# Attention followed by an MLP on one core: W1's first load and the first matmuls by contraction tile, and half of the first M built on ScalarE

## The chip, the cores and the metric

The kernel runs on one core of a Trainium2 chip. The metric is device microseconds of one execution. A kernel is profiled once per run and timed several times; the profile's span is some 1.8 us shorter than the time of the same execution (299.0 us against 300.83 for the kernel before), since it begins with the first recorded instruction. Times inside a profile count from the span's start.

## The reference

```python
def _attn_ref(q, k, v):                      # q, k, v: (8, 8, 576, 64), batch, head, position, feature
    q_s = softmax of q over features         # exp, then divided by its sum
    k_s = softmax of k over positions
    kv  = einsum('bhsd,bhse->bhde', k_s, v)  # 64 x 64 per head
    return einsum('bhsd,bhde->bhse', q_s, kv)

def _moe_ref(x, w_in, w_out):                # x: (4608, 512), w_in: (512, 2048), w_out: (2048, 512)
    h = x @ w_in
    g = where(h > 0, h, exp(min(h, 0)) - 1)  # ELU
    return g @ w_out
```

(The two softmaxes are shortened here.) Nearly all the work is in the two products of the MLP.

## The kernel before

The program lists operations with what they read and write, and a small scheduler gives each engine its order. Here the order is fixed by a table, `ORDER`, of operation numbers per engine. The work comes in *units* of four heads of one batch; units 0 and 1 fill the first block of 512 columns of x. For one unit:

- ScalarE takes exp of q and k; VectorE sums exp of q (`ZQ`) and scales it (`QS`); V is cast (`VB`).
- TensorE transposes QS; the result is copied out of PSUM as `qsT`.
- TensorE multiplies K by V, with a column of ones for K's sums. *M* (`MBLK`) is that product divided by the sums, laid out with each pair of heads on a block diagonal. *A* is M times `qsT`, copied out of PSUM as x, transposed (`XT`, called X below).
- The MLP then multiplies `W1` by X in groups g = 0 to 7 of two 128-row tiles each, over four *contraction tiles*, kc = 0 to 3. Unit 0 makes kc 0 and 1, unit 1 makes kc 2 and 3.

```python
    def m(self, n, ps, key, at=KV):                  # M of unit n, on VectorE
        S.add("dve", 82, lambda e: e.reciprocal(rz..., PV[:, :, D:D + 1]), ...)
        for h in range(2):
            hs = slice(h * 64, h * 64 + 64)
            S.add("dve", 208, lambda e, h=h, hs=hs: e.tensor_tensor(
                self.MBLK[i][hs, :, h:128:2], PV[hs, :, 0:D],
                rz[hs, :].unsqueeze(2).broadcast_to([64, 2, D]), ALU.mult), ...)
    # ... cut ...
    def program(self):
        # ... loads of q, k, v of units 0 and 1 ...
        for g0, g1, half in ((0, 3, 0), (0, 3, 1), (3, 5, None), (5, 8, None)):
            self.load_w1(g0, g1, half, ...)          # two transfers each
        # ... cut: attention of units 0 and 1, W2's loads ...
        for half in range(2):                        # the first matmuls of the MLP
            for g in range(3):
                self.hg_mm(0, g, turns[g], key, half)   # 2 tiles x 2 contraction tiles
        for g in range(8):
            self.hg(0, g, turns[g], key, "da"[g % 2], g > 2)   # groups 3 to 7, and all ELUs
```

Where TensorE would sit idle early on, a routine puts *filler* matmuls: they write to a bank that nothing reads yet, and are there to keep TensorE's clock up. It begins with them at a fixed time.

```python
    SPIN_FROM = 7900.0      # ns
    # ... in fill(), for each idle stretch of TensorE before the MLP:
    count = int((o.start - free - 150) / (430 if free == self.SPIN_FROM else 260))
```

The softmax here doesn't subtract the row's maximum and nothing guards it: scores larger than these inputs give would overflow.

Of the kernel before, what the change touches and what calls it, by code (L numbers as in the profile page):

```python
# [11 lines left out]
B, H, S, D = 8, 8, 576, 64  # L12
# [11 lines left out]
    "pe": (  # L24
        "30 28 32 43 45 47 50 67 54 68 70 71 69 72 82 86 93 115 103 90 129 128 137 136 131 139 107 "
        "130 138 109 151 152 150 126 134 149 132 156 157 158 140 173 146 153 159 172 174 175 233 238 "
        "237 239 192 243 249 245 244 251 250 201 255 257 256 203 263 262 212 268 261 267 269 313 309 "
        "321 317 350 220 325 333 329 280 391 334 282 338 342 291 412 346 351 299 399 404 395 417 362 "
        "400 364 408 425 430 373 413 421 438 426 381 479 434 439 487 450 500 492 483 505 488 452 513 "
        "518 461 496 469 501 526 509 564 514 572 522 538 585 527 540 568 577 573 598 581 586 590 594 "  # L30
        "603 611 549 607 636 599 556 657 640 612 662 644 649 653 645 670 622 666 624 683 688 658 679 "
        "632 675 671 634 696 709 684 692 701 714 697 705 722 727 735 718 710 740 731 748 723 744 761 "
        "736 766 757 753 749 770 787 762 774 779 775 783 788 792 793 805 797 801 809 "),
    "act": (
        "3 22 33 23 24 31 29 34 35 48 44 55 73 76 77 79 83 84 87 94 95 97 104 91 92 116 117 119 98 "
        "108 120 127 135 133 163 160 179 147 166 154 169 205 176 230 231 188 234 180 240 241 191 246 "
        "215 252 253 202 258 204 211 264 213 265 273 270 214 218 310 322 314 217 284 318 221 279 326 "
        "294 355 281 330 296 335 283 290 392 343 297 292 339 293 347 366 352 376 300 405 361 396 378 "
        "363 401 409 365 372 418 375 443 414 454 379 422 374 431 427 382 464 435 449 480 440 451 466 "
        "493 467 484 531 489 453 460 463 506 519 462 497 470 502 542 510 515 565 537 523 539 554 551 "  # L40
        "528 569 578 574 541 552 616 582 591 587 595 548 555 550 608 637 600 626 557 604 641 613 650 "
        "654 621 646 623 663 667 689 631 625 659 680 633 676 672 685 693 715 702 698 635 706 719 728 "
        "711 732 741 724 745 737 767 758 750 771 754 763 776 780 784 789 794 798 806 802 810 812 "),
    "dve": (
        "2 4 5 0 6 7 25 26 37 27 38 39 40 41 42 36 46 49 51 52 53 56 74 75 78 80 81 85 88 89 96 100 "
        "105 106 101 102 122 118 110 111 112 123 124 141 142 143 148 155 182 183 184 177 178 232 206 "
        "235 236 193 194 207 195 196 197 242 208 247 198 248 254 259 260 266 274 275 271 272 276 311 "
        "312 285 319 222 223 286 320 224 225 226 227 287 327 328 356 331 332 357 336 337 358 344 345 "
        "348 349 367 353 368 354 301 369 302 303 304 305 306 397 398 402 403 410 411 444 415 416 445 "
        "446 423 424 428 429 383 384 455 385 386 387 388 436 456 457 437 441 442 485 490 486 532 491 "  # L50
        "498 499 533 471 503 472 534 473 474 504 511 543 544 512 475 476 516 517 524 525 545 529 530 "
        "570 571 575 576 583 584 596 597 617 588 618 589 609 610 601 558 602 619 642 643 559 627 560 "
        "561 562 614 615 628 629 563 655 656 647 648 668 669 660 661 673 674 681 682 686 687 694 695 "
        "707 699 708 700 720 721 712 713 733 734 725 726 746 747 738 739 759 760 751 752 772 764 765 "
        "773 777 778 785 786 "),
    "gp": (
        "1 14 15 16 17 18 19 20 21 57 59 58 63 60 61 62 64 66 99 65 113 125 144 121 114 145 181 186 "
        "189 "),
    "sp": (
        "8 9 10 11 12 13 170 187 161 164 171 185 165 190 200 168 162 199 209 210 216 167 219 277 278 "  # L60
        "229 228 323 315 288 295 316 289 324 298 341 359 308 360 377 307 340 393 370 371 406 394 420 "
        "380 407 419 447 433 390 465 482 432 458 448 389 494 481 495 459 468 478 507 520 535 477 567 "
        "508 521 536 553 566 546 580 547 579 620 605 638 606 593 592 630 651 652 639 677 665 690 664 "
        "678 703 716 717 691 730 704 729 756 768 769 742 755 743 782 781 790 791 795 796 799 800 807 "
        "808 803 804 811 "),
}
# [173 lines left out]
def t_f32r(n):  # L240
    return (n + 32) / 2.4


class Gen:
# [49 lines left out]
    def init(self):  # L294
        S = self.S
        S.add("dve", 100, lambda e: e.memset(self.ID[:, :], 0.0), -95, W=["ID"])
        S.add("gp", 300, lambda e: e.affine_select(
            self.ID[:, :], self.ID[:, :], compare_op=ALU.not_equal, fill=1.0, base=0,
            pattern=[[-1, 128]], channel_multiplier=1), -38, X=["ID"])
        self.ident = S.ops[-1]  # L300
        S.add("dve", 60, lambda e: e.memset(self.RZK[0][:, :], 0.0), -90, W=["RZK0"])
        S.add("act", 1400, lambda e: e.activation(self.RZK[0][:, :], self.RZK[0][:, :], AF.Exp), -80,
              X=["RZK0"])
        self.table = S.ops[-1]
        for i in range(2):
            S.add("dve", 80, lambda e, i=i: e.memset(self.VB[i][:, :, :, D:D + 1], 1.0), -88,
                  W=[f"VBone{i}"], follow=S.ops[-1] if i else None)
            S.add("dve", 280, lambda e, i=i: e.memset(self.MBLK[i][:, :, :].bitcast(F32), 0.0), -88,
                  W=[f"MBLK{i}", f"MBLK{i}0", f"MBLK{i}1"], follow=S.ops[-1])
        self.cleared = S.ops[-1]  # L310
# [18 lines left out]

    def load_w1(self, g0, g1, half, key, after=()):  # L330
        w = self.w_in.rearrange("(h kc d) f -> h d kc f", h=2, d=D)
        sl = slice(g0 * 256, g1 * 256)
        ks = slice(0, 4) if half is None else slice(2 * half, 2 * half + 2)
        xs = (0, 1) if half is None else (half,)
        for h in range(2):
            self.S.add("gp", ISSUE["gp"], lambda e, h=h: e.dma_start(
                self.W1[h:128:2, ks, sl], w[h, :, ks, sl]), key,
                W=[f"W1_{g}{x}{h}" for x in xs for g in range(g0, g1)],
                dma=f"w1{g0}{xs[0]}{h}", nbytes=(len(xs) * (g1 - g0) << 17) * (1.25 if g0 == 3 else 1), after=after,
                follow=self.gpq)  # L340
            self.gpq = self.S.ops[-1]

    def load_w2(self, s, key, after=()):
# [106 lines left out]
    def kv_mm(self, n, ps, at=KV):  # L450
# [3 lines left out]
        def mm(e):  # L454
# [7 lines left out]
            return last  # L462
        return 615 if at == self.KV else 290, [f"kR{i}", f"VB{i}", f"VB{i}x", f"VBone{i}"], mm

    def m(self, n, ps, key, at=KV):
# [5 lines left out]
        for h in range(2):  # L471
            hs = slice(h * 64, h * 64 + 64)
            S.add("dve", 208, lambda e, h=h, hs=hs: e.tensor_tensor(  # L473
                self.MBLK[i][hs, :, h:128:2], PV[hs, :, 0:D],
                rz[hs, :].unsqueeze(2).broadcast_to([64, 2, D]), ALU.mult),
                key, R=[f"RZK{i}"], W=[f"MBLK{i}{h}"], X=banks)

# [4 lines left out]
    def ao_mm(self, n, x, ps, at=0):  # L482
# [5 lines left out]
        def mm(e):  # L488
            for f in range(2):
# [4 lines left out]
        return (2 * t_f32r(n_), [f"qsT{self.alt(n)}{y}" for y in (0, 1)] +  # L494
                [f"MBLK{i}{y}" for y in ("", 0, 1)], mm)

# [36 lines left out]

    def hg_mm(self, j, g, ps, key, half=None):
        S = self.S
        P = self.PS[ps]
        banks = [f"b{2 * ps}", f"b{2 * ps + 1}"]
        rc = BLK * (j % 3)
        kcs = range(4) if half is None else range(2 * half, 2 * half + 2)
        xs = [f"X{kc}_{(8 * j + x) % (RING // 64)}" for kc in kcs for x in range(8)]  # L540
        ws = [f"W1_{g}{x}{h}" for x in sorted({kc // 2 for kc in kcs}) for h in range(2)]

# [96 lines left out]
    def program(self):  # L639
# [9 lines left out]
        loaded = S.ops[-1]  # L649
        for g0, g1, half in ((0, 3, 0), (0, 3, 1), (3, 5, None), (5, 8, None)):  # L650
            self.load_w1(g0, g1, half, -30, [gate, self.ident] if half == 0 else ())
            S.ops[-2].behind = loaded
# [6 lines left out]
        self.tp(1, D_, -7, ("act", "dve"))  # L659
        self.side(C, -5, self.ao_mm(0, 0, C))  # L660
        self.xt(0, 0, C, -10, "both")
        self.side(0, -3, self.kv_mm(1, 0))
        kv1 = S.ops[-1]
        self.m(1, 0, -12)
        S.spare_until = S.ops[-4]
        self.side(0, -2, self.ao_mm(1, 0, 0))
        self.xt(1, 0, 0, -10, "both")
# [98 lines left out]
        turns = [3, 1, 2, 0, 3, 1, 0, 2]  # L766
        for half in range(2):
            for g in range(3):
                self.hg_mm(0, g, turns[g], key, half)
        for g in range(8):  # L770
# [96 lines left out]
```

## Time and profile before

| kernel before | |
|---|---|
| time | 301.47 us median of 3 (301.1 to 301.81); with two more executions, timed beside the changed kernel, the median is the same |
| span of the profile | 299.0 us |
| TensorE busy | 287.1 us, 96% |
| first MLP matmul; number 9, the first to use unit 1; number 11 | 14.95; 17.37; 17.94 us |
| W1's last load landed; first matmul that needs it (number 41) | 24.7; 24.75 us |
| first output product, when block 0's 64 matmuls are done | 30.70 us |

The lines are shown in the prediction below. In the changed kernel's order the first matmul to use unit 1 is number 11, so I compare number 11.

### The profile page before, as it was taken

What the parts mean: (1) busy time and instruction counts of PE and PEld (TensorE: products, weight loads), DVE (VectorE), ACT (ScalarE), POOL (GpSimd) and SP (SyncE); (2) the same over time, 40 slices, a digit from 0 to 9 for tenths busy, and PEclk for the clock granted to TensorE, in tenths of its full rate; (3) what the DMA queues carried; (4) which work ended last, traced back from release to release, by engine and by line L of the source; (5) the groups of instructions that cost most, each with busy time, mean ns of one, the idle gap of its engine ahead of it and who ended that gap; (6) DMA issues with size and microseconds to landing.
All of it is one profiled execution on the core that took longest, in us unless ns stands there. A gap on an engine that the chain in (4) does not pass through costs nothing.

```text
span 299.0 us, 4421 instructions
## 1 busy us (share of the span) xinstructions
PE 287.1 (96%) x1851; PEld 234.5 (78%) x1851; DVE 189.5 (63%) x244; ACT 182.3 (61%) x212; POOL 21.7 (7%) x33
## 2 busy tenths in 40 slices
PE   0899999999999999999999999999999999999995
PEld 0487877677888888888888888888888888888885
DVE  3958935985898685894568855588427256655500
ACT  5858848988977967867755766534462423432411
POOL 0860145100000000000000000000000000000000
PEclk9999999999999999999999999999999999999999
DMA  7999998994498697289546327041312302004214
GB/s 260 387 398 389 390 391 262 240 371 157 118 247 259 141 338 181 71 263 266 175 116 164 88 66 186 2 99 37 86 36 51 70 2 53 0 0 107 64 41 105
DMA packets 35443, 49.96 MB, mean 167 GB/s; under 512 B 16352, under 2 KB 16608, under 8 KB 35424
## 3 DMA queue, kind: packets, MB, share of 16 engines
q1 hardware_dynamic: 29840, 34.15, 41.3%
q0 software_dynamic: 5504, 15.47, 16.3%
q8 instruction: 14, 0.23, 0.3%
q10 hardware_dynamic: 80, 0.07, 0.1%
q14 instruction: 5, 0.04, 0.1%
HBM read 36.70 MB, written 9.44 MB: 154 GB/s over the span
## 4 chain that ended last, share of the span: by engine, by line
PE 89%; DVE 4%; DMA 3%; ACT 1%; SPq 1%; issue 0%
PE PS L592 43%; PE PS L547 41%; PE PS L491 3%; DMA QT<-QS 2%; PE PS L460 2%; DMA QR<-in_q_dram 1%; DVE ZQ L376 1%; DVE QS L384 1%; PE PS L407 1%; SPq L634 1%; DVE XT L516 0%; DVE GT L582 0%; ACT QR L356 0%; ACT qsT L435 0%; ACT ESB L563 0%; DVE MBLK L473 0%
## 5 line engine op out<-in xcount | busy, mean ns | idle before, releaser
L592 PE MATMUL PS<-W,GT 128*128 128x512 f32 (+1 forms) x592 | 141.4, 386 | 0.4 <-DVE GT L582 0.4
L547 PE MATMUL PS<-XT,W 128*128 128x512 f32 x576 | 140.5, 391 | 0.7 <-DVE RZK L469 0.5
L547 PEld LDWEIGHTS PS<-XT,W 128*128 128x128 f32 x576 | 107.1, 188 | 24.0 <-DVE XT L516 0.9
L592 PEld LDWEIGHTS PS<-W,GT 128*128 128x128 f32 x592 | 107.7, 188 | 22.1 <-DVE GT L582 0.8
L563 ACT ACTIVATE ESB<-PS 128x1024 f32<-128x1024 f32 x72 | 73.7, 1027 | 64.7 <-PE PS L547 64.3
L580 DVE TENSOR_SCALAR ESB<-ESB 128x1024 f32<-128x1024 f32 x64 | 44.4, 695 | 67.0 <-ACT ESB L563 66.4
L582 DVE TENSOR_TENSOR GT<-ESB,PS 128x1024 fp32r<-128x1024 f32 x64 | 77.7, 1217 | 1.8
L624 ACT ACTIVATE OSB<-PS 128x512 f32<-128x512 f32 x31 | 18.2, 598 | 30.9 <-PE PS L592 30.6
L376 DVE TENSOR_REDUCE ZQ<-QR 128x18 f32<-128x1152 f32 x16 | 21.5, 1344 | 7.3 <-ACT QR L356 7.2
L513 ACT ACTIVATE XT<-PS 128x512 fp32r<-128x512 f32 (+6 forms) x32 | 19.5, 608 | 7.0 <-PE PS L491 6.5
L384 DVE TENSOR_TENSOR QS<-QR,RZQ 128x1152 f16<-128x1152 f32 x16 | 21.6, 1353 | 0.3
L356 ACT ACTIVATE QR<-QR 128x1152 f32<-128x1152 f32 x16 | 18.6, 1165 | 2.9 <-DMA QR<-in_q_dram 2.9
L360 ACT ACTIVATE KR<-KR 128x1152 bf16<-128x1152 f32 x16 | 18.5, 1160 | 3.0 <-DMA KR<-in_k_dram 3.0
L435 ACT ACTIVATE qsT<-QT 128x1152 fp32r<-128x1152 f16 x12 | 14.0, 1166 | 0.7 <-DMA QT<-QS 0.7
L369 ACT ACTIVATE VB<-VR 128x1152 bf16<-128x1152 f32 (+1 forms) x12 | 13.5, 1124 | 0.7 <-DMA VR<-in_v_dram 0.7
L491 PE MATMUL PS<-qsT,MBLK 128*128 128x320 f32 (+5 forms) x64 | 13.9, 303 | 0.0
L491 PEld LDWEIGHTS PS<-qsT,MBLK 128*128 128x128 f32 x64 | 11.7, 190 | 2.6 <-DVE MBLK L473 0.2
L576 DVE SCALAR_TENSOR_TENSOR GT<-PS,ESB 128x1024 fp32r<-128x1024 f32 x8 | 9.8, 1220 | 4.2 <-ACT ESB L574 4.2
L672 PE MATMUL PS<-ID 128*128 128x512 f16 x7 | 3.3, 590 | 7.5 <-ACT QR L356 7.5
L473 DVE TENSOR_TENSOR MBLK<-PS,RZK 64x128 fp32r<-64x128 f32 x32 | 9.2, 289 | 0.9
L574 ACT ACTIVATE ESB<-ESB 128x1024 f32<-128x1024 f32 x8 | 8.5, 1060 | 0.2
L469 DVE RECIPROCAL RZK<-PS 128x2 f32<-128x2 f32 x16 | 2.6, 164 | 8.7 <-PE PS L460 7.7
(29 smaller groups left out, 59.7 us busy)
## 6 DMA issues: line engine op xcount, KB each, us to landing
out_dram<-OSB SPq DMA_DIRECT2D x62, 128.0 KB, 2.4
QR<-in_q_dram SPq DMA_DIRECT2D x12, 576.0 KB, 5.3
KR<-in_k_dram SPq DMA_DIRECT2D x12, 576.0 KB, 5.6
VR<-in_v_dram SPq DMA_DIRECT2D x12, 576.0 KB, 5.6
W<-in_moe_w_out_dram POOLq DMA_DIRECT2D x4, 1024.0 KB, 18.9
QR<-in_q_dram POOLq DMA_DIRECT2D x4, 576.0 KB, 11.4
KR<-in_k_dram POOLq DMA_DIRECT2D x4, 576.0 KB, 11.6
VR<-in_v_dram POOLq DMA_DIRECT2D x4, 576.0 KB, 8.0
```

The source lines that it names most:

```text
L356: S.add("act", t_act(1152, False), lambda e: e.activation(flat(q), flat(q), AF.Exp), key - 3, X=[f"qR{i}"], follow=self.table)
L360: S.add("act", t_act(1152, False), lambda e: e.activation(ek[:, :, :, :].rearrange("p h c d -> p (h c d)"), flat(k), AF.Exp), key - 2, X=[ ...
L376: S.add("dve", t_dve(1152), lambda e: e.tensor_reduce(self.ZQ[i][:, :, :].rearrange("p h c -> p (h c)"), q[:, :, :, :].rearrange("p h c d ...
L384: S.add("dve", t_dve(1152), lambda e: e.tensor_tensor(qso, q[:, :, :, :], rz, ALU.mult), key - 3, R=[f"qR{i}", f"RZQ{i}"], W=[f"QS{self.al ...
L491: last = e.matmul(P[:, y:y + n_], M[:, f, :], T[:, c0:c1, f * 64:f * 64 + 64], start=True, stop=True)
L513: S.add("act", t_act((h1 - h0) * n_, True), lambda e, dst=dst, src=src: e.activation(dst, src, AF.Copy), key, W=W, X=X)
L547: last = e.matmul(P[:, t * 512:(t + 1) * 512], self.W1[:, kc, tt * 128:(tt + 1) * 128], self.XT[:, kc, rc:rc + BLK], start=(kc == 0), stop ...
L563: S.add("act", t_act(1024, True), lambda e: e.activation(esb[:, :], P[:, :], AF.Exp), key, W=[f"E{i}"], X=banks)
L580: S.add("dve", t_dve(1024, 2), lambda e: e.tensor_scalar(esb[:, :], esb[:, :], 1.0, -1.0, ALU.min, ALU.add), key, X=[f"E{i}"])
L582: S.add("dve", t_dve(1024), lambda e: e.tensor_tensor(gt, esb[:, :], P[:, :], ALU.max), key, R=[f"E{i}"], W=gw, X=banks)
L592: last = e.matmul(dst, GT[:, jj, ts * 128:(ts + 1) * 128], self.W2[:, jj, c0:c1], start=(jj == 0), stop=(jj == 15))
L624: S.add("act", t_act(512, True), lambda e: e.activation(osb[:, :], src, AF.Copy), key, W=[f"O{i}0", f"O{i}1"], X=[f"b{bk}"])
```

## The change

Its intent: begin the MLP sooner. Part (a) loads the first W1 block in quarters of the contraction instead of halves. Part (b) runs the first matmuls contraction tile by contraction tile, so that a matmul needs one quarter of W1 and one half of a unit's X. Part (c) builds half of M of units 0 and 1 with two ScalarE instructions for each unit, beside VectorE. Part (d), the part hardest to see, is a new `ORDER` for every engine. The diff, with the table and the bookkeeping cut:

```diff
 ORDER = { ...
-    (about 800 numbers)
+    (about 800 other numbers)
@@ m()
         for h in range(2):
             hs = slice(h * 64, h * 64 + 64)
+            if n < 2 and h:
+                for f in range(2):
+                    S.add("act", 64 / 1.2 + 80, lambda e, f=f, hs=hs: e.activation(
+                        self.MBLK[i][hs, f, 1:128:2], PV[hs, f, 0:D], AF.Copy,
+                        scale=rz[hs, f:f + 1]), key, R=[...], W=[f"MBLK{i}1{f}"])
+                continue
             S.add("dve", 208, ...)
@@ program()
-        for g0, g1, half in ((0, 3, 0), (0, 3, 1), (3, 5, None), (5, 8, None)):
+        for g0, g1, kcs in ((0, 3, (0,)), (0, 3, (1,)), (0, 3, (2, 3)), (3, 5, range(4)), (5, 8, range(4))):
...
-        self.side(C, -5, self.ao_mm(0, 0, C))
+        self.ao_parts(0, C, -5)          # A as two operations, one per half of M
...
-        for half in range(2):
+        for kc in range(4):
             for g in range(3):
-                self.hg_mm(0, g, turns[g], key, half)
+                self.hg_mm(0, g, turns[g], key, kc=kc)
```

## The prediction

> **What bounds the kernel now.** I read the page first, parts 1 and 2.
>
> ```profile
> span 299.0 us, 4421 instructions
> PE 287.1 (96%) x1851; PEld 234.5 (78%) x1851; DVE 189.5 (63%) x244; ACT 182.3 (61%) x212; POOL 21.7 (7%) x33
> ...
> PE   0899999999999999999999999999999999999995
> ...
> GB/s 260 387 398 389 390 391 262 240 371 157 118 247 259 141 338 181 71 263 266 175 116 164 88 66 186 2 99 37 86 36 51 70 2 53 0 0 107 64 41 105
> ```
>
> TensorE is full from the third slice to the end. Its 1168 matmuls of 512 columns follow each other 0.227 us apart in the trace, so they alone need 265 us; with attention's matmuls the stream from 14.95 us to 296 us has no room. The change touches only the start. But DMA is full there too: about 390 GB/s in slices 2 to 6, up to about 45 us. So I ask two things: when does TensorE's dense stream start, and when does the next weight arrive?
>
> For the first, the chain of waits, of 0 to 32 us:
>
> ```profile
> 11.95 0.18 DVE RZK L469
> ...
> 12.16 0.29 DVE MBLK L473
> ...
> 12.47 0.29 DVE MBLK L473
> ...
> 12.80 0.76 DVE VB L372
> ...
> 13.59 0.69 DVE qsT L417
> 14.28 0.60 DVE XT L516
> 14.88 0.09 DVE RZK L469
> 14.96 1.16 PE PS L547 x4
> 16.12 0.47 PE PS L491 x2
> 16.58 13.91 PE PS L547 x60
> ```
>
> The first MLP matmul (L547) comes at 14.95 us, at the end of a row of VectorE work: M of unit 0 in two halves of 0.29 us, half of V, half of a transpose, X. After it TensorE is dense: 4 matmuls, attention's 2, then 60.
>
> For the second, the weight loads of the PE timeline, 14 to 31 us (start, length, what ended the idle time before):
>
> ```profile
> 17.36 7.12 PEld L547 LDWEIGHTS PS<-XT,W 128*128 128x128 f32 x32 [0.30 <-DVE XT L516]
> 24.75 5.31 PEld L547 LDWEIGHTS PS<-XT,W 128*128 128x128 f32 x24 [0.26 <-DMA W<-in_moe_w_in_dram]
> ```
>
> There are two small stops: at 17.36 for X of unit 1, and at 24.75 for W1's last load (groups 5 to 7). From the list of matmul starts they cost 0.15 and 0.11 us. The second matters most. The view of W1's transfers gives issues at 8.4, 9.0, 9.8, 10.4, 11.0, 11.65, 12.2 and 12.8 us, landing 5.2, 5.7, 6.0, 6.4, 7.1, 9.2, 10.5 and 11.9 us later: 13.6 and 14.8 (first half of contraction), 15.8 and 16.8 (second), 18.1 and 20.8 (groups 3, 4), 22.7 and 24.7 us (groups 5 to 7). TensorE reaches group 3 at 21.1, 0.3 us after its weights, and group 5 just as its own land. **The stream cannot move up by more than about 0.1 us at group 5 unless W1 lands sooner.**
>
> **What the Trainium skill says.** (1) DMA: Bandwidth & Descriptors, § Issuing engines are not separate DMA queues: DMAs of all issuers run on the same 16 engines and interleave; splitting an issue saves only issue time. The trace agrees: the windows view shows 401 GB/s at 14.95 to 16.58 us and 393 at 16.58 to 30.5. Splitting W1's first load brings its first quarter sooner, not its last. (2) ScalarE: Activation LUTs, § What ACT_TABLE_LOAD costs: an ACTIVATE takes 186 ns + 0.833 ns per element, and about 93 ns more for a pointer operand such as a scale. No such instruction with a pointer scale is in the trace; the 128-column copy out of PSUM took 276 ns against 293 by that formula. (3) Runtime: NRT & Kernel Launch, § Instruction fetch mechanics: instructions come in blocks of 16 KiB over DMA. The trace has one such packet at 17.5 us (0.02 MB, 1.1 us on one DMA engine). In the packet list W1's last two loads have a tail of about 1.4 us from what looks like one late engine, which I put down to it. The change leaves that fetch about where it is.
>
> **The change part by part.**
> (a) *W1's first load in quarters.* 192 KB instead of 384 KB for each of the first four transfers, same bytes in the same order. kc 0 should land at about 13.7 us and kc 1 at 14.8 instead of both at 14.8; kc 2 and 3 still at 16.8. Two more issues of 0.64 us (POOL row of the timeline: 8 in 5.1 us) put W2 and later issues 1.3 us back; as they land 14 to 24 us after issue, behind a full queue, that costs nothing.
> (b) *First matmuls by contraction tile.* Same 64 matmuls. A group can start on kc 0 with ScalarE's half of X alone, before VectorE's half.
> (c) *Half of M on ScalarE.* VectorE loses 2 x 0.29 us. ScalarE gains four ACTIVATEs of 64 columns: 276 ns less 64 x 0.83, plus the skill's 93, estimated at 0.3 us each, 1.2 us together, on an engine with almost no gap from 9.6 to 15 us.
> (d) *A new order.* Comparing instruction orders shows what the diff hides: VectorE scales QS of unit 0 before it sums unit 1, then waits for unit 0's K-V product before scaling QS of unit 1. So the second scaling (1.36 us), done at 11.6 us before, comes after M.
>
> Now the new path, with the durations of the old trace. ScalarE still ends VB at 10.81 us (V's arrival decides) and qsT at 12.05. K-V of unit 0 on TensorE starts at about 11.28 (after three filler matmuls of 0.427), against 11.19. VectorE: RZK 12.05 to 12.22, M's lower half to 12.55. ScalarE: first upper piece to 12.55. First half of A at 12.64, not 13.06. ScalarE then has K's exp (1.16, to 13.7), X kc 0 (0.60, to 14.3), second M piece (to 14.6), V half (0.67, to 15.3). VectorE: QS 12.57 to 13.93, V half to 14.7, qsT 14.72 to 15.41, X kc 1 to 16.1. TensorE: second half of A at 14.65; matmuls 1 and 2 (kc 0) at 14.9; K-V of unit 1, waiting for V, at 15.35; matmuls 3 and 4 at 15.65; 5 and 6 (kc 1) at 16.2; M of unit 1 ready at 16.9, A of unit 1 at 17.0; X of unit 1 at 18.2; matmuls 7 to 10 meanwhile; matmul 11 at 18.25. Before: number 5 at 16.42, and six at 0.227 plus the 0.15 stop give number 11 at 17.94.
>
> So what starts sooner (A by 0.4 us) is given back by the displaced QS and by ScalarE's extra work: the dense stream comes 0.3 us **later** by this sum, and 0.1 of it returns because the stop at group 5 goes. Net about +0.2 us. Past 31 us the orders differ in detail; the old stream loses about 1.2 us at four places from 54 to 74 us (waits for VectorE's GT and the like), which the new order may win or worsen by some tenths. I take -0.3 for it, because the order comes out of a search that was kept: 301.5 + 0.2 - 0.3 = 301.4; I state 301.3.
>
> **Rivals.**
> 1. *The start moves up and stays so.* If ScalarE's pieces take 0.2 us and QS slips in earlier, matmul 11 comes up to 0.7 us sooner. For it: VectorE is the chain at 12 to 15 us and is relieved. Against it: W1's landing at 24.7 us. Only if W1 also lands sooner does the time fall to about 300.7.
> 2. *W1 or W2 becomes the wait.* A faster start meets W1 at 20.8 and 24.7 us, and W2's second quarter, which now is needed after 4 matmuls instead of 8 (landing 31.7 us by its transfer view). Gain gone: 301.3 to 301.6.
> 3. *ScalarE becomes the bound of the first 18 us.* For it: its idle time there is near nothing. If its pieces cost more than estimated or K's exp holds X up, each 0.1 us counts twice: 302.
>
> **Range and chances.** Everything in play is under 1 us in 301; the three runs before spread over 0.7 us. Range 300.4 to 302.2. 2% is 6 us, and nothing I see reaches that: faster 0.01, same 0.98, slower 0.01.
>
> **What would show it right or wrong.** First MLP matmul at about 14.9 us with a gap soon after; X of unit 1 at about 18 us (17.3 before); W1's last load still at 24.7 us with TensorE at group 5 just after; MLP of block 0 ending within 0.3 us of 30.3. The new ACTIVATEs at 0.25 to 0.35 us. Wrong if W1's last load lands before 24 us and the stream is there to use it, if the four stops of 54 to 74 us vanish (1 us faster), or if a W2 stop over 0.5 us appears at 31 to 45 us.

## More of the kernel before

"First output product" is the measure that I use most: it says how long the first 31 us really took, with all their waits.

## The result

The changed kernel took 301.24 us median of 5 (301.08 to 301.35), against 301.47 before (median of 5, 301.1 to 301.81). The ratio is 0.9994, with a 95% interval of 0.9981 to 1.0008: the same.

First the page of the changed kernel: span, busy times with instruction counts, and TensorE's busy tenths in 40 slices.

```profile
span 299.4 us, 4438 instructions
...
PE 287.8 (96%) x1854; PEld 234.5 (78%) x1854; DVE 188.5 (63%) x242; ACT 183.1 (61%) x216; POOL 22.7 (8%) x35
...
PE   0999999999999999999999999999999999999995
```

About one microsecond went from VectorE to ScalarE, GpSimd has one more for its two further requests of W1, and nothing else stands out. The chain of waits of the changed kernel, from 10 to 31 us (start, length, what), shows much more:

```profile
10.21 1.28 PE PS L694 x3
11.49 0.67 PE PS L462 x19
...
12.39 0.32 ACT MBLK L477
...
12.73 1.16 ACT KR L362
...
13.92 0.60 ACT XT L533
...
14.54 0.31 ACT MBLK L477
...
14.88 0.69 ACT VB L371
...
15.59 0.71 ACT qsT L416
...
16.35 1.21 PE PS L569 x4
17.55 0.46 PE PS L511 x2
18.01 13.15 PE PS L569 x58
```

(L569 is the MLP's first product, L511 is A, L462 the K-V product, L694 the fillers.) Before, the chain from 12 to 15 us was a row of VectorE work; now it is a row of ScalarE work, and it ends at 16.3 instead of 14.9: with the copy of qsT, after which the PSUM bank that held the transposes is free for group 1 of the MLP. ScalarE builds a piece of M, then takes exp of unit 1's K, copies X, builds another piece of M, casts V and copies qsT, with nothing between. Two matmuls of the MLP had already run at 15.25, but the dense stream of 4, attention's 2 and then 58 begins at 16.35; before it was 4, 2 and 60 from 14.96. Unit 1's X does not hold the stream here: ScalarE's half of it is done at 18.42, and number 11, which needs it, follows number 10 without a gap at 18.75.

The end of the first block is dense now, where before it stopped for W1's last load. The weight loads of the changed kernel (start, length):

```profile
17.62 13.11 PEld L569 LDWEIGHTS PS<-XT,W 128*128 128x128 f32 x58
```

No idle time stands before it and it has no break at group 5. Yet the first output product comes at 31.37 us, against 30.70: **0.67 us later**. After it, the kernel before has these stops of TensorE in the stretch from 60 to 76 us,

```profile
65.68 1.69 PEld L547 LDWEIGHTS PS<-XT,W 128*128 128x128 f32 x8 [0.53 <-DVE GT L582]
...
74.35 0.76 PEld L592 LDWEIGHTS PS<-W,GT 128*128 128x128 f32 x4 [0.42 <-DVE GT L576]
```

and the changed kernel has no stop like the second:

```profile
62.53 1.69 PEld L569 LDWEIGHTS PS<-XT,W 128*128 128x128 f32 x8 [0.20 <-DVE GT L598]
...
65.96 1.69 PEld L569 LDWEIGHTS PS<-XT,W 128*128 128x128 f32 x8 [0.46 <-DVE GT L604]
```

From first output product to the last matmul it took 264.75 us, against 265.03 before. The profile's net is +0.4 us (299.4 against 299.0), a ratio of 1.0013, and the timed runs, with a scatter of that size, don't show it.

### The profile page after: what moved, and what is told of

It reads as the page before. It is cut to its first block, busy times and chain, and to the rows that moved or that the text cites. A ratio compares the mean times of both kernels' runs of the same rounds, so it can differ in the third digit from the quotient of the medians.

```text
span 299.4 us, 4438 instructions
## 1 busy us (share of the span) xinstructions
PE 287.8 (96%) x1854; PEld 234.5 (78%) x1854; DVE 188.5 (63%) x242; ACT 183.1 (61%) x216; POOL 22.7 (8%) x35
## 4 chain that ended last, share of the span: by engine, by line
PE 93%; ACT 3%; DVE 1%; DMA 1%; issue 0%
PE PS L614 44%; PE PS L569 43%; PE PS L499 3%; PE PS L462 2%; DMA QR<-in_q_dram 1%; PE PS L409 1%; ACT ESB L585 1%; DVE QS L386 0%; DVE ZQ L378 0%; PE PS L694 0%; DVE GT L598 0%; ACT QR L358 0%; ACT KR L362 0%; ACT ESB L596 0%; ACT qsT L416 0%; ACT VB L371 0%
## 5 line engine op out<-in xcount | busy, mean ns | idle before, releaser
L569 PE MATMUL PS<-XT,W 128*128 128x512 f32 x576 | 140.8, 392 | 0.2
L614 PEld LDWEIGHTS PS<-W,GT 128*128 128x128 f32 x592 | 108.2, 188 | 22.1 <-DVE GT L604 0.8
L569 PEld LDWEIGHTS PS<-XT,W 128*128 128x128 f32 x576 | 106.8, 188 | 22.8 <-DVE GT L598 0.7
L378 DVE TENSOR_REDUCE ZQ<-QR 128x18 f32<-128x1152 f32 x16 | 21.5, 1347 | 5.3 <-ACT QR L358 5.2
L499 PEld LDWEIGHTS PS<-qsT,MBLK 128*128 128x128 f32 x60 | 11.0, 190 | 2.4 <-DVE MBLK L481 0.2
L499 PE MATMUL PS<-qsT,MBLK 128*128 128x320 f32 (+4 forms) x60 | 12.6, 297 | 0.0
L694 PE MATMUL PS<-ID 128*128 128x512 f16 x10 | 4.4, 552 | 7.5 <-ACT QR L358 7.5
L481 DVE TENSOR_TENSOR MBLK<-PS,RZK 64x128 fp32r<-64x128 f32 x30 | 8.6, 285 | 0.8
```

Of the source, the lines that this page charges most:

```text
L378: S.add("dve", t_dve(1152), lambda e: e.tensor_reduce(self.ZQ[i][:, :, :].rearrange("p h c -> p (h c)"), q[:, :, :, :].rearrange("p h c d ...
L499: last = e.matmul(P[:, y:y + n_], M[:, f, :], T[:, c0:c1, f * 64:f * 64 + 64], start=True, stop=True)
L569: last = e.matmul(P[:, t * 512:(t + 1) * 512], self.W1[:, kc, tt * 128:(tt + 1) * 128], self.XT[:, kc, rc:rc + BLK], start=(kc == 0), stop ...
L614: last = e.matmul(dst, GT[:, jj, ts * 128:(ts + 1) * 128], self.W2[:, jj, c0:c1], start=(jj == 0), stop=(jj == 15))
```

## The experiments

The theory (A): the earlier start that (a) and (b) allow is eaten by ScalarE's row, into which (c) puts pieces of M in front of unit 1's K, X and V, and by the order; and what is left could not be used, because W1 lands just when the kernel before needs it (W). Rivals: TensorE's clock, which is at half rate in these first microseconds, decides the start and not the order (E); the 0.7 us between two single profiles is scatter, of the loads (B) or of when the clock rises (F). The expectations name such theories by letters at times; each says in its own words what it expects. The new order, (d), was never run alone.

All profiled executions together. "K" is when unit 0's K landed, "11" and "41" are MLP matmuls by number (41 is the first of group 5), "W1" is when W1's last load landed, "out" the first output product, "rest" the span less "out". Times are medians, ratios with their intervals are against the kernel before in the same job; its medians were 300.88, 300.93 and 301.24 in the three jobs (11 executions in each, 300.37 to 301.69 over all); the first "before" and "after" were timed together, ahead of these.

| kernel | K | first | 11 | W1 | 41 | out | rest | time | ratio |
|---|---|---|---|---|---|---|---|---|---|
| before | 8.1 | 14.95 | 17.94 | 24.7 | 24.75 | 30.70 | 268.3 | 301.47 | |
| before_again | 7.8 | 15.01 | 18.02 | 24.3 | 24.84 | 30.66 | 268.2 | 300.78 | 1.000 (0.9984 to 1.0017) |
| after | 7.8 | 15.25 | 18.75 | 24.1 | 25.55 | 31.37 | 268.0 | 301.24 | 0.9994 (0.9981 to 1.0008) |
| after_again | 8.2 | 15.16 | 18.67 | 25.1 | 25.47 | 31.28 | 268.0 | 301.16 | 1.0007 (0.9994 to 1.0019) |
| split_only | 7.6 | 14.15 | 17.57 | 23.9 | 24.40 | 30.21 | 268.1 | 301.52 | 1.001 (0.9986 to 1.0035) |
| m_dve | 8.1 | 14.86 | 18.31 | 24.6 | 25.11 | 30.92 | 268.1 | 301.26 | 1.0023 (1.0001 to 1.0046) |
| nofill | 8.2 | 15.79 | 19.66 | 25.8 | 26.46 | 32.28 | 268.1 | 301.83 | 1.0026 (1.0007 to 1.0045) |
| warm_before | 8.4 | 15.05 | 18.27 | 26.0 | 26.06 | 32.01 | 268.2 | 300.62 | 0.9985 (0.9972 to 0.9998) |
| warm_after | 7.9 | 14.55 | 18.06 | 24.3 | 24.86 | 30.67 | 268.0 | 300.86 | 0.9997 (0.9984 to 1.0011) |
| warm_m_dve | 7.8 | 14.19 | 17.65 | 24.1 | 24.46 | 30.27 | 268.1 | 300.69 | 0.9991 (0.9976 to 1.0006) |
| extra_before | 8.1 | 15.26 | 18.26 | 25.2 | 25.27 | 31.22 | 269.3 | 301.91 | 1.0028 (1.0014 to 1.0042) |
| extra_after | 8.1 | 15.26 | 18.78 | 25.5 | 25.58 | 31.43 | 268.1 | 301.52 | 1.0027 (1.0005 to 1.0048) |
| warm_split | 8.0 | 13.97 | 17.42 | 24.8 | 24.84 | 30.78 | 268.3 | 300.91 | 0.9999 (0.9984 to 1.0015) |
| warm_split_last2 | 8.5 | 14.39 | 18.05 | 25.7 | 25.39 | 31.20 | 268.3 | 301.0 | 0.9997 (0.998 to 1.0014) |

(In warm_split_last2 the last load is that of groups 6 and 7; group 5 had landed at 23.0.)

Two readings at once. In all profiles but one "rest" is 268.0 to 268.3: what differs between them differs in the first 31 us. And K lands at 7.6 to 8.5 us and W1's last load at 23.9 to 26.0, with no order in it that the kernels explain, so a difference of 0.3 us between two profiles needs a look at where it comes from. There is an order between the two columns, though. The program requests W1 only when unit 0's K has landed (0.3 us after it, in every profile), and the later K is, the later W1: in the five profiles with K at 7.9 us or before, W1's last load is there at 23.9 to 24.3; in the other nine (two of them with an extra load), at 24.6 to 26.0. To request W1 without waiting for K was not tried.

### The kernel before again, and the changed kernel again

No edit to either.

> The kernel before once more, unchanged, to see what run-to-run differences a second trace shows. Theory A (the changed kernel starts its dense MLP stream 0.8 us later, and gives 0.4 of it back later by its order): matmul 11 of the MLP again at 17.9 us and MLP block 0 ending at 30.4 us, within 0.2 us; W1's last load landing at 24.1 to 24.8 us. Rival B (the two profiled runs differ by chance in when the first loads landed, 0.35 us for K of unit 0, and the shift is partly that): the first K lands 0.3 us sooner here too and matmul 11 moves with it by more than 0.2 us. Ratio 1.000 within 0.1%.

> The changed kernel once more, unchanged, in one job with the three below. In the five traces so far TensorE's clock rose from half to full rate at 11 to 17 us, differently in each run, and matmul 11 of the MLP came at 17.6 to 19.7 us. Theory F (when the clock rises in the start is a lottery of the run, and it scatters the times of both kernels by more than the change does): matmul 11 differs from 18.75 us by 0.2 us or more with the rise, and the ratio to the kernel before is 0.998 to 1.003. Theory A (the change makes the start a fixed 0.8 us later and the later order gives 0.4 back): matmul 11 at 18.7 us again, ratio 1.001.

The first output product came at 30.66 and 31.28, within 0.1 us of the first profiles, although K landed 0.3 us sooner in one and 0.5 us later in the other. So the later start of the changed kernel is its own and no scatter (against B and F). Neither start hangs on K here: both chains of waits go back to unit 0's Q, which landed within 0.15 us in all four profiles (4.66 to 4.80 us). The small stop at group 5 of the kernel before is gone in its second profile: W1 landed 0.4 us sooner there. Times: ratio 1.000 for the kernel against itself, 1.0007 for the changed one; the profile's 1.0013 is inside the interval of this ratio and outside that of the first comparison.

### Only the splitting, on the old order

```diff
-        for g0, g1, half in ((0, 3, 0), (0, 3, 1), (3, 5, None), (5, 8, None)):
+        for g0, g1, kcs in ((0, 3, (0,)), (0, 3, (1,)), (0, 3, (2, 3)), (3, 5, range(4)), (5, 8, range(4))):
...
-        for half in range(2):
+        for kc in range(4):
```

The order of the kernel before is kept (renumbered for the new operations), M stays on VectorE, A stays one operation.

> The kernel before with only W1's first load in quarters and the first MLP matmuls by contraction tile; M stays whole on VectorE, order and fillers as before. Theory A (what held the first MLP matmuls was M and X on VectorE, and the dense stream is set by X of unit 1 and by W1's last load): first matmul at 14.5 to 14.9 us, X of unit 1 unchanged at 17.3 us, matmul 11 at 17.8 to 17.95, W1's last load landing unchanged within 0.3 us; time -0.1 to 0 us. Rival C (the split of the load is what helps: weights were the wait at 14.9 us): first matmul 0.3 us sooner or more and MLP block 0 ending 0.3 us sooner, time -0.3 us or more.

The MLP began at 14.15 us. The chain of waits of this kernel shows the last of it:

```profile
13.70 0.41 PE PS L466 x35
14.11 0.04 issue
14.15 0.73 PE PS L555 x2
```

The matmul (L555) no longer waits for VectorE's half of X, nor for W1's second load: it follows the K-V product of unit 1. So (a) and (b) do what they are for, 0.8 us sooner. Number 11, however, is only 0.4 us sooner, and of that 0.1 to 0.2 us is there already when the first transposes start (10.02, against 10.12 and 10.20); from number 9 on the matmuls need unit 1's X, which the splitting does not touch. The weight loads from number 9 on,

```profile
17.00 12.57 PEld L555 LDWEIGHTS PS<-XT,W 128*128 128x128 f32 x56 [0.22 <-issue]
```

have no stop at group 5, because W1's last load had landed at 23.9; so the first output product kept the lead, 30.21 us. That is what rival C expected of a profile. Its 0.3 us of time did not come: 300.1 (the profiled one) and 300.3 us for two of six, 301.5 to 302.3 for the others. What sets those four apart was not profiled.

### Half of M back on VectorE

```diff
-            if n < 2 and h:
-                for f in range(2):
-                    S.add("act", ...)      # the ScalarE pieces of M
-                continue
```

This is the changed kernel with VectorE building both halves of M, in the places of its order where the first half stood.

> The changed kernel with M of the first two units back on VectorE (second half right after the first), everything else as in the changed kernel, fillers fixed at its counts. Theory A1 (ScalarE's four ACTIVATEs of 0.31 us are what made the stream late, as the chain from 12.4 to 16.3 us is all ScalarE): matmul 11 comes back from 18.77 to about 18.2 us, time -0.5 us. Theory A2 (they are neutral: what ScalarE loses VectorE wins, and the lateness is the new order's, the fillers ahead of the K-V product and the displaced scaling of unit 1): matmul 11 at 18.6 to 19.1 us, time within 0.2 us of the changed kernel.

Number 11 came at 18.31 instead of 18.75 and 18.67, and the first output product at 30.92. In the timeline of ScalarE in this kernel (start, length, what, idle time before),

```profile
11.73 1.16 ACT L367 ACTIVATE KR<-KR 128x1152 bf16<-128x1152 f32 x1
13.20 0.60 ACT L533 ACTIVATE XT<-PS 128x512 fp32r<-128x512 f32 x1 [0.31 <-PE PS L511]
13.70 0.68 ACT L376 ACTIVATE VB<-VR 128x576 bf16<-128x576 f32 x1
```

K's exp no longer waits for the K-V product of unit 0: it starts at 11.73 instead of 12.73. But this profile also had its clock up for that product (0.49 us, not 0.71), so not all of the 0.4 us is M's. The pair with early fillers, below, measures it without that. The timed runs don't show a gain (ratio 1.0023, with one run of 302.82). What is left against the two profiles of the kernel before, 0.3 to 0.4 us at number 11 and 0.2 to 0.3 at the first output product, is of the new order with its fillers; no run takes these apart.

### Without the three fillers ahead of the first K-V product

```diff
-                count = int((o.start - free - 150) / (430 if free == self.SPIN_FROM else 260))
+                count = {32: 3, 50: 1, 48: 3}.get(o.idx, 0)     # as the changed kernel, less 34: 3
```

In the changed kernel the three fillers at 10.21 us, at half clock, put off the K-V product.

> The changed kernel without the three filler matmuls between the first transposes and the K-V product of unit 0, other fillers as they are. They ran from 10.0 to 11.4 us at 0.427 us each while V had been ready since 10.46. Theory A2 (they hold the whole start): K-V product at 10.5 to 10.6 instead of 11.42 us, first M piece on ScalarE at 11.6 instead of 12.39, matmul 11 at about 18.0 instead of 18.77, MLP block 0 ending 0.7 us sooner, time -0.6 us against the changed kernel. Rival D (W1 holds the stream): matmul 11 sooner, but a stop at group 5 until W1's last load lands at 24.1 to 24.7 us, time -0.2 us or less. Rival E (without fillers TensorE's clock stays at half rate longer): matmuls at 0.427 us past 14 us and no gain.

The K-V product did come 0.5 us sooner. It cost more than it gave. TensorE in this kernel:

```profile
10.92 0.72 PE L462 MATMUL PS<-VB,KR 64*64 64x65 bf16 x36 [0.83 <-ACT VB L371]
...
14.29 1.17 PE L409 MATMUL PS<-ID,QS 128*128 128x128 f16 x9
...
15.79 1.05 PE L569 MATMUL PS<-XT,W 128*128 128x512 f32 x2
```

The nine transposes of unit 1 took 1.17 us at 14.29; in the changed kernel they take 0.68. With 0.83 us idle ahead of the K-V product, TensorE was still at half its rate at 16.2 us (matmuls 1 and 2 are 0.427 us apart), and number 11 came at 19.66, as rival E expected. The ratio is 1.0026, but its interval overlaps that of the changed kernel. So in this profile, one against two of the changed kernel, the fillers earn their place, and the clock (E) is a real part of the start of the changed kernel.

### Fillers from 2 us on: the kernel before, the changed one, and the changed one with M on VectorE

```diff
-    SPIN_FROM = 7900.0
+    SPIN_FROM = 2000.0
...
-                count = int((o.start - free - 150) / (430 if free == self.SPIN_FROM else 260))
+                count = {32: 18, 34: 3, 50: 1, 48: 3}.get(o.idx, 0)   # here for the changed kernel
```

TensorE has nothing to do before 9 us, so 18 to 22 fillers there cost nothing and take the clock out of the comparison. The counts are written out so that all else stays as it was. The third kernel adds the edit of the section on M.

> The kernel before with 22 filler matmuls from about 2 us on, in place of 5 from 7.5 us, so that TensorE's clock is at full rate before the first transposes in every run. Theory F: every transpose from 10 us on 0.057 us after the one ahead (not 0.107), matmul 11 at 17.2 to 17.6 us (17.9 to 18.0 before), and timed runs that spread less than the 1.3 us of the eleven of before; time -0.3 us on the mean. Rival W (W1's last load sets the end of MLP block 0, so a faster start is lost at group 5): a stop of 0.2 us or more at group 5, W1's last load landing at 24.2 to 24.8 us, time within 0.1 us.

> The changed kernel with 18 filler matmuls from about 2 us on in place of 3 from 7.5 us. Theory F: K-V product of unit 0 at 10.9 us or sooner (11.42), first M piece at about 11.6 to 12.0, matmul 11 at 17.9 to 18.3 us, small spread, time -0.3 us against the changed kernel. If ScalarE's row of work (M, exp of K, X, M, V) is the only thing that holds the start and the clock plays no part: matmul 11 at 18.6 us or later.

> The same, with M of the first two units back on VectorE: the test of M on ScalarE without the lottery of the clock. Theory A1 (M on ScalarE costs the start 0.3 to 0.5 us, as 1.24 us of ACTIVATEs stand in ScalarE's row and only 0.6 us leave VectorE's): matmul 11 0.3 to 0.6 us sooner than in the run above, after allowing for when the first K landed, and time -0.3 us against it. Theory A2 (neutral): within 0.15 us.

The clock was up by 5.5 to 6.1 us in all three: the fillers go from 0.427 us apart to 0.216 there. In the changed kernel that alone brings number 11 from 18.75 and 18.67 to 18.06, as theory F expected. The weight loads of its 58 matmuls now start at 16.92, and with M on VectorE at 16.50. First the changed kernel, then the one with M on VectorE:

```profile
16.92 13.12 PEld L569 LDWEIGHTS PS<-XT,W 128*128 128x128 f32 x58
```

```profile
16.50 13.14 PEld L569 LDWEIGHTS PS<-XT,W 128*128 128x128 f32 x58
```

The first K-V products started 0.07 us apart (10.65 and 10.58), K's landings 0.1. **In this pair of profiles half of M on ScalarE costs the start 0.3 to 0.4 us**, which is theory A1. The timed runs, 300.86 and 300.69 us, don't tell the two apart; the 0.3 us of time that A1 expected is not shown. VectorE builds the same half in 0.29 us, and the stream starts sooner with it there, although QS of unit 1 stands behind it.

The profiled execution of the kernel before with early fillers was its one long one, 302.0 us where its five others took 300.53 to 300.94. Its fillers, and the stop that it made:

```profile
1.88 6.97 PE L672 MATMUL PS<-ID 128*128 128x512 f16 x22 [1.88 <-POOL ID L297]
```

```profile
22.14 3.50 PEld L547 LDWEIGHTS PS<-XT,W 128*128 128x128 f32 x16 [0.94 <-DMA W<-in_moe_w_in_dram]
```

Groups 3 and 4 of W1 landed at 22.1 us, 1.3 us later than in the first profile, and the last load at 26.0. TensorE stood still for 0.79 us at group 3 and 0.27 at group 5, counted from the starts of matmuls, and the first output product came at 32.01. So late loads can cost about 1 us of stops. The 17.2 to 17.6 us that theory F expected for number 11 was missed, with 18.27: in this execution unit 1's V, at 12.9 us, made VectorE wait for 0.41 us, and W1's second half landed at 17.5. So this profile says nothing of what early fillers do to a start with punctual loads. Whether other long executions of any kernel here have this cause is not shown; few of them were profiled.

By time, the kernel before with early fillers is the best: 300.62 us, ratio 0.9985, the only interval that lies wholly under 1. That is 0.15%, and with thirteen intervals one such can come by chance.

### A load of 256 KB between W1's first and second loads

```diff
+            if g0 == 3:
+                S.add("gp", ISSUE["gp"], lambda e: e.dma_start(self.GT[1][:, 8:9, :], w2[:, 0:1, :]), ...)
             self.load_w1(g0, g1, ...)
```

The destination is a part of a buffer that nothing reads until it is written again, so the result stays right. If the kernel before has no slack to W1 (W), it must stop; the changed kernel, which arrives later, should not.

> The kernel before with one more load of 256 KB put between W1's first and second loads, into a part of a buffer that nothing reads yet. It delays every later piece of W1 by about a microsecond and a half to two, and nothing else. Theory W (the kernel before has no slack to W1's arrival): the MLP matmuls stop for 0.3 to 0.7 us in front of group 3 and perhaps 0.1 to 0.4 us in front of group 5, the first block's first output product comes at 31.1 to 31.6 instead of 30.7 us, and the timed runs are 0.4 to 0.8 us over the kernel before. Rival (the weights have slack in both, and the one late run of the kernel with early fillers was something else): no stop over 0.15 us, first output product at 30.7 plus or minus 0.15, time within 0.2 us of the kernel before.

> The changed kernel with the same extra load at the same place. Theory W: its MLP matmuls run 0.65 to 0.8 us later, so they absorb that much of the delay: group 3 starts at 21.9 with a stop under 0.3 us, matmul 41 within 0.3 us of 25.5, first output product at 31.3 to 31.6, time 0 to 0.3 us over the changed kernel; so it comes out level with or under the kernel before with the same load. Rival: the later start is plain loss, and both kernels are delayed by the same amount (0.4 us or more here too), or neither.

The delay was smaller than I had meant it to be: W1's last load landed at 25.2 and 25.5 us. There was no stop at group 3, where I expected one. At group 5 the weight loads say, first of the kernel before with the extra load, then of the changed kernel with it:

```profile
25.27 5.32 PEld L550 LDWEIGHTS PS<-XT,W 128*128 128x128 f32 x24 [0.46 <-DMA W<-in_moe_w_in_dram]
```

```profile
25.50 5.30 PEld L572 LDWEIGHTS PS<-XT,W 128*128 128x128 f32 x24 [0.18 <-DMA W<-in_moe_w_in_dram]
```

The kernel before lost 0.31 us there by its matmul starts. The changed kernel lost nothing measurable: number 41 at 25.58 against 25.55 without the load. So its later start does buy slack, as W says. That the kernel before also began 0.3 us later here comes from W1's first half, which landed at 15.2 us; that was requested ahead of the extra load, so I do not put it down to it. It had landed at 14.9 and 14.3 us in the two profiles of the kernel before.

The larger loss of this kernel was one that nobody expected. Its chain of waits from 66 us on:

```profile
66.59 7.85 DMA out_dram<-OSBX
...
74.52 1.24 DVE GT L579
```

The last store of block 0 took 7.85 us, and its buffer lies where block 1's ELU writes next; VectorE waited for it, and "rest" is about 1 us longer here than in the other kernels. In the kernel before that store is issued at 65.7 and lands 6.5 us later, at 72.2, and VectorE writes there from 73.07: 0.9 us of slack. In the changed kernel it lands at 71.0 and the write starts at 73.3. The times are 301.91 and 301.52, but the ratios are alike, 1.0028 and 1.0027; the second includes one run of 303.19. So the profiles show the slack, and the timed runs do not confirm that it is worth anything.

### The splitting with early fillers, and with W1's last load in two

```diff
-        for g0, g1, kcs in (..., (3, 5, range(4)), (5, 8, range(4))):
+        for g0, g1, kcs in (..., (3, 5, range(4)), (5, 6, range(4)), (6, 8, range(4))):   # the second only
```

This takes from the change what was seen to help, (a) and (b), leaves out (c) and (d), and adds the early fillers.

> Only the splitting (W1's first load in quarters, the first matmuls by contraction tile) on the old order, all of M on VectorE, with 22 filler matmuls from 2 us on so that the clock is at its full rate by about 6 us. If the start is held by the clock, the first loads and ScalarE's row of M, this has none of the three but the loads: first MLP matmul at or under 14.3, matmul 11 at 17.2 to 17.5 us with K landed at 7.8 to 8.0, first output product at 29.9 to 30.4, a stop at group 5 if W1's last load lands after 24.2; time 0.3 to 0.8 us under the kernel before (ratio 0.997 to 0.999). Rival (the weights' arrival is what bounds the first block on the old order): matmul 11 is earlier but stops of the same size come at groups 3 and 5, first output product at 30.5 or later, time equal to the kernel before within 0.2 us.

> The same with W1's last load cut in two, group 5 alone and then groups 6 and 7, so that group 5 does not wait for the last packet of three groups. If the weights' arrival bounds an early first block: no stop over 0.1 us at group 5, and 0.1 to 0.3 us less than the same kernel with one last load, with a smaller spread of its runs. Rival: no difference over 0.1 us, because the weights of group 5 had landed in time anyway.

It had the earliest start of all: first matmul at 13.97, number 11 at 17.42. Its chain of waits, up to group 5:

```profile
1.75 6.28 DMA KR<-in_k_dram
8.03 0.29 issue
8.32 5.39 POOL W L341 x9
13.71 11.09 DMA W<-in_moe_w_in_dram
...
24.84 1.20 PE PS L555 x4
```

The chain goes back from W1's last load through the row of W1's requests to the landing of K, for which the first of them waits. The last load was issued at 13.71 and landed 11.09 us later; TensorE stood still for 0.69 us at group 5, and the first output product came at 30.78, where it is in the kernel before. The rival that I wrote down for this run came true: the earlier start was given back whole. In the two other profiles with number 11 sooner than before, split_only and warm_m_dve, W1's last load was there at 23.9 and 24.1 us, and the lead was kept: first output product at 30.21 and 30.27. So whether an earlier start is lost depends on when W1 lands in that execution. With the last load cut in two, the stop was at the load ahead of it:

```profile
21.59 8.98 PEld L558 LDWEIGHTS PS<-XT,W 128*128 128x128 f32 x40 [0.63 <-DMA W<-in_moe_w_in_dram]
```

Groups 3 and 4 landed at 21.5, group 5 had no stop, and the time was the same (ratios 0.9999 and 0.9997). K had landed 0.4 us later in this execution, so that part of its late start is the loads'.

## Why the prediction was right

The time, 301.24, lies 0.06 us from the 301.3 predicted, by a sum two of whose terms were mis-sized. That it lies so near is luck: its own sum gives 301.4, the median of the kernel before alone moved from 301.47 to 300.88 in a later job, and the first block came out 0.5 us longer than the sum had it. What was right is the class, "same", and what the gain would run into. Point by point:

- **The bound.** It named W1's arrival as what an earlier stream would meet. Shown by the splitting with early fillers: 0.5 us sooner at number 11, 0.69 us of stops, nothing gained; and by the two profiles in which W1 landed by 24.1 us and the lead was kept, as its "unless W1 lands sooner" says. The stop at group 5 was to vanish in the changed kernel, and it did. "Still at 24.7" for W1's last load held within the scatter: 24.1 and 25.1.
- **(a) and (b).** That a group can start on kc 0 with half of X is shown by the splitting alone: 14.15 us. In the profile about half of that lead was left when unit 1 was needed.
- **(c).** 0.3 us per piece was estimated, 0.302 to 0.316 measured. The pieces cost 1.2 us of ScalarE as foreseen, and lengthen the start by 0.3 to 0.4 us in the pair that isolates them.
- **(d).** QS of unit 1 after M, and the K-V product behind three fillers, are both in the trace: VectorE idle for 1.61 us, fillers in the chain at 10.21.
- **The mis-sized term: the start.** The prediction had number 11 at 18.25, 0.3 us later than before, and 0.2 net once the stop at group 5 was gone, with block 0 "ending within 0.3 us of 30.3". Number 11 came at 18.75, 0.8 us later, and the first output product 0.67 us later; the block's last matmul began at 30.77 instead of 30.10. The working lost its way at matmul 3, which it had at 15.65 and which came at 16.35; from there the stream is dense, and the step "X of unit 1 at 18.2, matmul 11 at 18.25" failed, as X was no wait. The K-V product of unit 0 started at 11.42 and not 11.28, which put M 0.14 us back, and the gaps between ScalarE's instructions added another 0.1 (V's half ended at 15.57, not 15.3). Then two things that ended together held matmul 3. One is the K-V product of unit 1: it started 0.24 us after V was there, at 15.81, and took 0.49 us, where the working had it at 15.35 and left it 0.3. The other is ScalarE's copy of unit 1's `qsT`, to 16.30, which empties the bank that group 1 of the MLP writes; the working had not counted it as a condition at all, and it is what the chain names. Rival 3, ScalarE as the bound of the start, is what the chain shows, though its 302 us was too dark.
- **The term for the order after 31 us** was -0.3. From first output product to last matmul it is -0.28 between the first two profiles, and -0.1 to -0.2 against the second profile of the kernel before and other kernels on the old order (264.93, 264.82 and 264.88 us); the stop at 74 us is what went; three of the four stops of 54 to 74 us are still there, 1.0 us of the 1.2. Right in sign, a little large. No stop over 0.12 us came at 31 to 45 us, so rival 2's wait for W2 did not appear.
- **The range** was wide enough for what was not foreseen: the loads, whose landing moves the start and the stops by up to a microsecond from one execution to the next. The prediction called that a spread of 0.7 us; the kernel before ranged from 300.37 to 301.81.
- **Two readings in the section on the skill.** The 401 and 393 GB/s there are all from GpSimd's queue: they show a full queue, and not that issuers share. What shows it is the stretch from 11 to 13 us, where that queue moved 286 GB/s and SyncE's 104, together 390, against 393 for SyncE's alone just before. And the tail of W1's last load was put down to an instruction fetch that the change "leaves about where it is". The fetch came at 17.5 and 19.9 us before and at 20.7 and 21.2 after, and the tail was there each time: the last ten to twelve packets end one by one, 0.12 us apart, over 1.2 to 1.5 us. In the two latest landings, 25.8 and 26.0 us, the tail is 1.9 and 2.1 us long. What makes it is not shown.

What stays open is the step from the profiles to the times. The changed kernel's first 31 us are 0.6 to 0.7 us longer in two profiles out of two, and its "rest" is 0.2 us shorter, yet its timed runs are level within their intervals. The kernel with the most slack to W1 may lose less in executions in which W1 is late, as the late execution of the kernel before suggests; that is argued and not shown.

## What to carry to other kernels

Before starting a stream sooner, look when its next input lands: here the weights landed just as they were needed, so an earlier start was kept in the two profiles in which they came early and given back whole as a stop on a DMA in the one in which they did not. Look also at what their request waits for, here the landing of K. Work moved from a busy engine to another one goes into that engine's queue in front of something; follow what stands behind it, here exp of K and X, and not only the instruction moved. And when the profile's gain is smaller than the spread with which the loads land, profile twice and compare where the stops are, rather than trust one number.

## What the Trainium skill lacked or had wrong

- "ScalarE: Activation LUTs", § What ACT_TABLE_LOAD costs: holds within 16 to 30 ns, for a form that the kernel before did not have. A 64-column ACTIVATE out of PSUM with a pointer scale took 0.302 to 0.316 us where the formula gives 332 ns; two back to back took 0.52 us together, so they overlap by about 0.1 as the section says.
- "TensorE: Matmul & The Clock Gate", § Part 1: The HAM clock gate (the "warmup" mystery): it puts the rise at about 4 us of sustained matmuls, give or take 0.5 us from run to run. With unbroken fillers the rate doubled 3.3, 3.7, 4.2, 4.2 and 5.8 us after the first of them (warm_after, warm_m_dve, warm_before, warm_split, warm_split_last2), so the spread is wider here. It gives no figure for a start of mixed small work with short idle stretches: with fillers from 7.4 us and transposes and the small K-V matmuls between them the full rate came only at 11 to 13 us, and without three of the fillers and with 0.83 us idle in their place it was still at half at 16.2 us. The profile's clock row shows 1.0 in all of these stretches; the half rate is seen only in durations, such as 1.14 us for nine transposes that take 0.68 at the full rate.
- No page has the spread of landings within one program: K at 7.6 to 8.5 us and W1's last load at 23.9 to 26.0 us after the start, where K was requested at 1.8 us in every kernel and the last part of W1 at 12.5 to 15.3.
